# Convolution bands loaded from raw taps and softmaxed on the chip; small inputs asked for first

## The chip, the cores and the metric

The kernel runs on one core of a Trainium2 chip. The metric is the device time of one launch in microseconds, the median of several runs; lower is better. TensorE (PE) multiplies matrices, VectorE (DVE), ScalarE (ACT) and GpSimd (POOL) work element by element, SyncE (SP) issues most of the DMA transfers. ACT and POOL issue some as well, each on a queue of its own.

## What is computed

`x` is (8, 3584, 192), float32. A causal convolution with 7 taps runs along the sequence, with one set of taps for each of 8 heads of 24 channels; the taps are softmaxed first. Each of the 28672 rows then goes through one of 8 experts (192 to 1024 to 192, ReLU), which is chosen by a gate with a bias that depends on the row's modality.

```python
w = exp(weight - max(weight)); w = w / (sum(w) + 1e-9)         # (8 heads, 7 taps)
y[b, s, h] = sum_k w[h, k] * x_padded[b, s + k, h]             # causal: 6 zeros ahead
logits = y @ w_gate + modality_bias[modality_id]               # (28672, 8)
e = argmax(logits); gate = softmax(logits)[e]
out = gate * (relu(y @ w1[e]) @ w2[e])
```

## The kernel before

The sequence is cut into blocks of 120 positions for each of the 8 batches. 4 batches of a block are a quad, and 19 groups of 1, 2 or 4 quads go through the first stage. For one group: `x` is loaded with 128 positions on the partitions (120 and a halo of 8); the convolution is a matmul with a band matrix (`band`, 128x120 for each head, lines 336 to 374 of the listing of before: `convolve_pair` makes two heads at a time in one PSUM tile `cv`, which is copied to `y`). `turn` transposes `y` on DVE, `gate` multiplies it with the gate matrix (`gt`), `logits` adds the bias, `choose` takes the largest (`top`, `ex`, `rk`, `oh`), `place` counts the rows of each expert with matmuls (`rp`) and makes the row numbers `idx`, and `send` scatters the rows of `y` to a DRAM buffer sorted by expert (`routed_rows`), 120 rows in one instruction of POOL. The groups are laid out one behind the other by generators (`all_groups`, `body`, `finish`).

The second stage walks over slots of the sorted rows: a slot loads the weights of its expert, and each pass of 256 rows goes through `first` (`hps`) and `second` (`po`). Slot 0 starts when the rows of the first four groups (20 scatters) have landed; from there the later groups run between the steps of the second stage.

What lies around the change is the start. The framework sets the order on each engine from the program, and `issue_after` holds an instruction behind another on its engine. On SP stand, in this order: the taps, `x` of group 0, the line of tap weights, the band in two halves of four heads, `x` of group 1, and six more loads of `x` that wait for the band (`behind_band`). The taps are softmaxed on one partition (DVE and ACT), written into a zeroed line per head (`line`, in `raw1`), the line goes to DRAM (`tap_lines`), and the band is read back from there with a step of one element from partition to partition, so that each partition holds the taps one place further. `load_modality` asks for the modality ids on POOL; `make_gate` builds the gate matrix in two forms, `wg_whole` (in float32, for the groups below 8) and `wg_parts` (high and low halves, from group 8 on); `make_modality` turns the ids into `mt` (two transposes on PE into a PSUM tile of the same ring of four that `cv` uses, and a copy on DVE); `make_bias` makes `first_bias` from `mt` on POOL. POOL also clears the lower rows of the four `y` buffers (`clear`). `warm` keeps PE busy with matmuls of ones until the band is there.

Of the kernel before, what the change touches and what calls it, by code (L numbers as in the profile page):

```python
# [12 lines left out]
I32 = mybir.dt.int32  # L13
# [18 lines left out]
WARM = 34  # L32
WAIT = 3
PAD = 64
# [15 lines left out]
def conv_then_routed_ffn(ctx, tc, x, weight, modality, w_gate, mod_bias, w1, w2, out):  # L50
# [61 lines left out]

    spark = const.tile([1, 1], F32, name="spark")
# [27 lines left out]
    def make_bands():  # L141

        wide = P + MB
        line = raw1[0][0:1].rearrange("p c n -> p (c n)")[:, 0:H * wide].rearrange("p (h u) -> p h u", h=H)
        nc.vector.memset(line, 0.0)
        least = const.tile([1, H], F32, name="least")
        nc.vector.memset(least, 1e-9)
        taps = const.tile([1, H, K], F32, name="taps")
        nc.sync.dma_start(out=taps, in_=weight.unsqueeze(0))
        peak = const.tile([1, H], F32, name="peak")  # L150
        nc.vector.tensor_reduce(out=peak, in_=taps, axis=AX.X, op=ALU.max)
        nc.vector.tensor_tensor(out=taps, in0=taps, in1=peak.unsqueeze(2).broadcast_to([1, H, K]), op=ALU.subtract)
        nc.scalar.activation(out=taps, in_=taps, func=AF.Exp)
        tot = const.tile([1, H], F32, name="tot")
        nc.vector.tensor_reduce(out=tot, in_=taps, axis=AX.X, op=ALU.add)
        nc.vector.tensor_tensor(out=tot, in0=tot, in1=least, op=ALU.add)
        nc.vector.reciprocal(out=tot, in_=tot)

        first = MB - 1 + HALO - K + 1
# [20 lines left out]
    def make_gate():  # L180


        wg = const.tile([P, NK, E], F32, name="wg")
        for q in range(P // Q):
            nc.scalar.dma_start(out=wg[q * Q:(q + 1) * Q], in_=w_gate.rearrange("(k c) e -> c k e", c=Q))
# [4 lines left out]
        nc.gpsimd.memset(whole, 0.0)  # L190
        parts = const.tile([P, NK, P], F32R, name="wg_parts")
        nc.vector.tensor_copy(out=parts, in_=whole)
        for q in range(P // Q):
            rows = slice(q * Q, (q + 1) * Q)
            nc.vector.tensor_copy(out=whole[rows, :, q * Q:q * Q + E], in_=wg[rows])
            state["wg"] = nc.vector.tensor_copy(out=parts[rows, :, q * Q:q * Q + 2 * E], in_=f(wgs[rows])).ins
        return whole, parts

    def make_modality():
        both = const.tile([MB, 2, E], F32, name="both")  # L200
        nc.scalar.dma_start(out=both.rearrange("p m e -> p (m e)"),
                            in_=mod_bias.rearrange("m e -> (m e)").partition_broadcast(MB))
# [10 lines left out]
        with tc.issue_after(state["wg"]):  # L213
            nc.vector.tensor_copy(out=mt.rearrange("p b s -> p (b s)"), in_=mt_ps.rearrange("p q r -> p (q r)"))
# [3 lines left out]
    def load_modality():  # L218
        half = NB // 2
        each = half * NSB  # L220
        room = raw2[1].rearrange("p c d -> p (c d)")
        ids = room[0:each, 0:4 * MB].bitcast(I32).rearrange("p (q s) -> p q s", q=2)
        words = modality.bitcast(I32)
        nc.vector.memset(room[0:1, 0:2 * CUT], 0.0)

        def rows_of(b0, b1, sb0, q):
            at = 2 * ((q * half + b0) * S + sb0 * MB - CUT)
            n = NSB - sb0
            dims = [[2 * S, b1 - b0], [2 * MB, n], [1, 2 * MB]] if sb0 == 0 else [[2 * MB, n], [1, 2 * MB]]
            nc.gpsimd.dma_start(out=ids[b0 * NSB + sb0:b1 * NSB, q], in_=bass.AP(words.tensor, words.offset + at, dims))  # L230

        nc.gpsimd.dma_start(out=ids[0:1, 0, 2 * CUT:], in_=words[0:2 * (MB - CUT)].unsqueeze(0))
        rows_of(0, 1, 1, 0)
        rows_of(1, half, 0, 0)
        rows_of(0, half, 0, 1)
        return room, ids, each

    modality_rows = load_modality()
# [27 lines left out]
    def make_bias(dst, n, ids):  # L266
# [4 lines left out]
        nc.gpsimd.tensor_tensor(out=dst, in0=dst, in1=start_row.unsqueeze(1).broadcast_to([MB, n * nb, E]), op=ALU.add)  # L271
# [286 lines left out]
    def all_groups():  # L558
# [345 lines left out]
    for y in y_bufs[1:]:  # L904
        clear(y)
# [176 lines left out]
```

## Time and profile before

| | us |
|---|---|
| median of three runs (lowest, highest) | 1234.53 (1234.31, 1235.81) |
| the profiled execution | 1234.43 |
| its span, from the first instruction to the last | 1232.6 |
| PE busy in the span | 1211.1 (98%) |
| DVE, ACT, POOL busy | 967.9, 723.3, 528.7 |

The span begins with the first instruction. Times in the rows are microseconds from there. PE is counted as busy whenever a matmul is in flight, so its share tells that there is little air between matmuls, and not that each of them runs at its peak. The chain of the page, followed back from the last instruction, lies on PE for 84% of the span.

### The profile page before, as it was taken

To read this page: it belongs to the slowest core of one execution; us is meant where nothing else is said; L and a number is where in the kernel's file an instruction comes from. 1 tells how busy PE (TensorE), PEld (TensorE's weight loads), DVE (VectorE), ACT (ScalarE), POOL (GpSimd) and SP (SyncE) were. 2 spreads that over 40 slices of the span, in tenths; PEclk is the share of its full clock that TensorE was granted. 3 is DMA by queue.
4 is the path that set the end of the run, shared out by engine and by line. 5 is a ranking of instruction groups with operands and counts; after the bars stand their busy time and mean duration, and the time that the engine had idled before them with its cause. 6 is when DMAs were issued, how large, how long until landed. Compare 5 with 4: busy or idle time off the path is not lost.

```text
span 1232.6 us, 27980 instructions
## 1 busy us (share of the span) xinstructions
PE 1211.1 (98%) x9220; PEld 1196.6 (97%) x9220; DVE 967.9 (79%) x2455; ACT 723.3 (59%) x1588; POOL 528.7 (43%) x549
## 2 busy tenths in 40 slices
PE   9899999999999999999999999999999999999996
PEld 7799999999999999999999999999999999999995
DVE  6788986888788888788778887777766666787894
ACT  2366655565666556666655666555555555566773
POOL 7756564636344343545445344344352122112221
PEclk9999999999999999999999999999999999999998
DMA  8897563345544354345532554233262344943271
GB/s 222 221 224 211 122 179 77 77 116 142 134 88 111 84 125 110 72 107 142 143 63 57 109 121 126 53 71 61 73 158 56 81 106 106 258 112 94 42 191 38
DMA packets 308448, 144.29 MB, mean 117 GB/s; under 512 B 222922, under 2 KB 294930, under 8 KB 308293
## 3 DMA queue, kind: packets, MB, share of 16 engines
q1 hardware_dynamic: 284574, 97.83, 36.7%
q0 software_dynamic: 22752, 44.54, 11.6%
q8 instruction: 74, 1.21, 0.4%
q14 instruction: 81, 0.66, 0.2%
q10 hardware_dynamic: 967, 0.03, 0.0%
HBM read 116.58 MB, written 51.82 MB: 137 GB/s over the span
## 4 chain that ended last, share of the span: by engine, by line
PE 84%; DVE 6%; DMA 3%; issue 3%; ACT 1%; POOL 1%; SPq 0%; POOLq 0%; DVEq 0%; ACTq 0%
PE hps L835 39%; PE po L855 25%; PE po L859 12%; PE gt L405 3%; PE cv L349 3%; PE cv L365 2%; DMA routed_rows<-y,idx 1%; DVE hl L839 1%; DVE w1b L110 1%; DMA xr<-in_x_dram 1%; ACT lowp L871 1%; DVE xl L110 1%; DVE w2b L110 1%; POOL out_dram L874 0%; DVE sxs L822 0%
## 5 line engine op out<-in xcount | busy, mean ns | idle before, releaser
L855 PE MATMUL po<-w2b,hh 128*128 128x384 f32 x1824 | 556.3, 355 | 0.0
L835 PE MATMUL hps<-sxh,w1b 128*128 128x256 f32 x1824 | 482.0, 287 | 3.2 <-DVE hl L839 2.0
L839 DVE SCALAR_TENSOR_TENSOR hl<-hps,hh 128x512 fp32r<-128x512 f32 x456 | 312.0, 686 | 193.9 <-ACT hh L838 191.2
L838 ACT ACTIVATE hh<-hps 128x512 fp32r<-128x512 f32 x456 | 272.7, 598 | 324.6 <-PE hps L835 319.1
L859 PE MATMUL po<-w2b,hl 128*128 128x192 f32 x1824 | 443.4, 253 | 0.0
L874 POOL DMA_INDIRECT out_dram<-o,tags x228 | 236.5, 1037 | 382.5 <-DVE o L873 320.3
L251 POOL DMA_INDIRECT routed_rows<-y,idx x240 | 262.3, 1093 | 300.4 <-DVE hl L839 146.8
L835 PE MATMUL hps<-sxs,w1b 128*128 128x256 f32 x1824 | 363.5, 281 | 0.4 <-DVE sxs L822 0.4
L835 PEld LDWEIGHTS hps<-sxh,w1b 128*128 128x128 f32 x1824 | 344.8, 189 | 8.5 <-DVE hl L839 8.0
L859 PEld LDWEIGHTS po<-w2b,hl 128*128 128x128 f32 x1824 | 346.2, 191 | 0.0
L855 PEld LDWEIGHTS po<-w2b,hh 128*128 128x128 f32 x1824 | 344.3, 189 | 0.7 <-DVE o L873 0.4
L835 PEld LDWEIGHTS hps<-sxs,w1b 128*128 128x128 f32 x1824 | 280.0, 189 | 0.7 <-issue 0.7
L835 PE MATMUL hps<-sxl,w1b 128*128 128x256 f32 x912 | 256.3, 281 | 0.0
L835 PEld LDWEIGHTS hps<-sxl,w1b 128*128 128x128 f32 x912 | 173.0, 190 | 0.0
L110 DVE TENSOR_TENSOR w1b<-raw,w1b 128x512 fp32r<-128x512 f32 x152 | 101.3, 676 | 6.2 <-ACT w1b L108 5.9
L871 ACT ACTIVATE lowp<-po,tags 128x192 f32<-128x192 f32 x228 | 83.5, 417 | 30.9 <-PE po L855 30.8
L108 ACT CAST w1b<-raw 128x512 fp32r<-128x512 f32 x152 | 92.8, 621 | 3.4 <-DMA raw<-in_moe_w_dram 2.6
L110 DVE TENSOR_TENSOR w2b<-raw,w2b 128x384 fp32r<-128x384 f32 x152 | 80.9, 542 | 8.0 <-ACT w2b L108 7.6
L873 DVE SCALAR_TENSOR_TENSOR o<-po,tags,lowp 128x192 f32<-128x192 f32 x228 | 84.5, 412 | 2.2 <-ACT lowp L871 2.2
L820 ACT CAST sxs<-tp 64x128 fp32r<-64x128 f32 x224 | 66.7, 298 | 30.1 <-DVE tp L795 27.4
L108 ACT CAST w2b<-raw 128x384 fp32r<-128x384 f32 x152 | 75.9, 512 | 1.1
L822 DVE TENSOR_TENSOR sxs<-tp,sxs 64x128 fp32r<-64x128 f32 x224 | 64.8, 289 | 8.6
(158 smaller groups left out, 966.4 us busy)
## 6 DMA issues: line engine op xcount, KB each, us to landing
raw<-in_moe_w_dram SPq DMA_DIRECT2D x38, 768.0 KB
raw<-in_moe_w_dram SPq DMA_DIRECT2D x38, 512.0 KB
raw<-in_moe_w_dram SPq DMA_DIRECT2D x76, 256.0 KB
near<-routed_rows SPq DMA_DIRECT2D x208, 64.0 KB
xr<-in_x_dram SPq DMA_DIRECT2D x32, 384.0 KB
x<-in_x_dram SPq DMA_DIRECT2D x26, 384.0 KB
routed_rows<-filler SPq DMA_DIRECT2D x9, 776.0 KB
far<-routed_rows SPq DMA_DIRECT2D x208, 32.0 KB
```

The lines of the kernel that those rows point to most:

```text
L108: nc.scalar.copy(out=hi, in_=raw)
L110: return nc.vector.tensor_tensor(out=lo, in0=raw, in1=f(hi), op=ALU.subtract).ins
L251: state["scatter"] = nc.gpsimd.indirect_dma_start(out=scr, out_offset=bass.IndirectOffsetOnAxis(ap=idx, axis=0), in_=src, in_offset=None,).ins
L820: nc.scalar.copy(out=hi, in_=raw)
L835: nc.tensor.matmul(hps[:, u, :], wa[:, c, fs], mv[z], start=n == 0, stop=n == len(terms) - 1)
L838: nc.scalar.activation(out=hh, in_=hps, func=AF.Relu)
L839: hl_ins = nc.vector.scalar_tensor_tensor(out=hl, in0=hps, scalar=0.0, in1=f(hh), op0=ALU.max, op1=ALU.subtract)
L855: nc.tensor.matmul(po, hh[:, u, js], wb[:, c, :], start=c == 0, stop=c == NF - 1, skip_group_check=True)
L859: nc.tensor.matmul(po[:, 0:D], hl[:, u, js], wb[:, c, 0:D], start=False, stop=False, skip_group_check=True)
L871: nc.scalar.activation(out=lowp, in_=po[:, D:2 * D], func=AF.Copy, scale=gate)
L873: turn_behind(nc.vector.scalar_tensor_tensor(out=o, in0=po[:, 0:D], scalar=gate, in1=lowp, op0=ALU.mult, op1=ALU.add))
L874: st = nc.gpsimd.indirect_dma_start(out=out, out_offset=bass.IndirectOffsetOnAxis(ap=tag.bitcast(I32)[:, j, 1:2], axis=0), in_=o, in_offse ...
```

## The change

The ids, the taps, the gate matrix and the biases are asked for ahead of all else: the ids on POOL, the other three on ACT. The line in DRAM no longer holds softmaxed taps between zeros. It holds the raw weights, copied from DRAM to DRAM, between values of -1e30 that come from a small tile on 8 partitions (`outer`). The band is read from it in four parts of two heads. On the chip each head then goes through an exponential with minus the largest tap as bias (`peak`, ACT, in place), and each pair of heads is multiplied with one over the sum (`tot`, DVE). For that the taps are also loaded to all 128 partitions, where `peak` and `tot` are made. The padding turns to zero in the exponential.

`mt` is copied behind the last of these multiplications, the four copies into `wg_whole` stand behind `mt`, and `wg_parts` is made when group 5 is laid out, behind the row numbers that are newest there. The three clears of `y` stand behind `first_bias`. There are 28 warm matmuls, and 34 before.

```diff
-WARM = 34
+WARM = 28
+PARTS = 5
...
+    modality_rows = load_modality()
+
+    taps = const.tile([P, H, K], F32, name="taps")
+    nc.scalar.dma_start(out=taps.rearrange("p h k -> p (h k)"), in_=weight.rearrange("h k -> (h k)").partition_broadcast(P))
+    wg = const.tile([P, NK, E], F32, name="wg")
+    for q in range(P // Q):
+        state["wg"] = nc.scalar.dma_start(out=wg[q * Q:(q + 1) * Q], in_=w_gate.rearrange("(k c) e -> c k e", c=Q)).ins
+    both = const.tile([MB, 2, E], F32, name="both")
+    nc.scalar.dma_start(out=both.rearrange("p m e -> p (m e)"), in_=mod_bias.rearrange("m e -> (m e)").partition_broadcast(MB))
     spark = const.tile([1, 1], F32, name="spark")
...
     def make_bands():
...
+        first = MB - 1 + HALO - K + 1
+        each = first + K
+        outer = raw1[0][0:H, 0, 0:first]
+        nc.vector.memset(outer, -1e30)
+        lines = nc.dram_tensor("tap_lines", (H, 2 * each), F32, kind="Internal").ap()
+        nc.sync.dma_start(out=lines[:, first:each], in_=weight)
+        nc.sync.dma_start(out=lines.rearrange("h (two u) -> h two u", two=2)[:, :, 0:first],
+                          in_=outer.unsqueeze(1).broadcast_to([H, 2, first]))
+        band = xp.tile([P, H, MB], F32, name="band", tag="xr_0")
+        for h in range(0, H, 2):
+            part = bass.AP(lines.tensor, h * 2 * each, [[1, P], [2 * each, 2], [1, MB]])
+            state["band"] = nc.sync.dma_start(out=band[:, h:h + 2], in_=part).ins
+        peak = const.tile([P, H], F32, name="peak")
...
-        state["line"] = nc.vector.tensor_tensor(out=line[:, :, first:first + K], in0=taps,
-                                                in1=tot.unsqueeze(2).broadcast_to([1, H, K]), op=ALU.mult).ins
-        lines = nc.dram_tensor("tap_lines", (H, wide), F32, kind="Internal").ap()
-        nc.sync.dma_start(out=lines.unsqueeze(0), in_=line)
-        band = xp.tile([P, H, MB], F32, name="band", tag="xr_0")
-        for q in range(2):
-            part = bass.AP(lines.tensor, q * H // 2 * wide, [[1, P], [wide, H // 2], [1, MB]])
-            state["band"] = nc.sync.dma_start(out=band[:, q * H // 2:(q + 1) * H // 2], in_=part).ins
+        state["line"] = nc.vector.reciprocal(out=tot, in_=tot).ins
+        for h in range(H):
+            nc.scalar.activation(out=band[:, h], in_=band[:, h], func=AF.Exp, bias=peak[:, h:h + 1])
+            if h % 2:
+                pair = slice(h - 1, h + 1)
+                state["tuned"] = nc.vector.tensor_tensor(out=band[:, pair], in0=band[:, pair], in1=tot[:, pair].unsqueeze(2).broadcast_to([P, 2, MB]), op=ALU.mult).ins
...
     def make_gate():
...
+        with tc.issue_after(state["mt"]):
+            for q in range(P // Q):
+                rows = slice(q * Q, (q + 1) * Q)
+                nc.vector.tensor_copy(out=whole[rows, :, q * Q:q * Q + E], in_=wg[rows])
...
+        def make_parts():
+            with tc.issue_after(state["idx"]):
+                nc.vector.tensor_copy(out=parts, in_=whole)
+            for q in range(P // Q):
+                rows = slice(q * Q, (q + 1) * Q)
+                nc.vector.tensor_copy(out=parts[rows, :, q * Q:q * Q + 2 * E], in_=f(wgs[rows]))
...
-        with tc.issue_after(state["wg"]):
-            nc.vector.tensor_copy(out=mt.rearrange("p b s -> p (b s)"), in_=mt_ps.rearrange("p q r -> p (q r)"))
+        with tc.issue_after(state["tuned"]):
+            state["mt"] = nc.vector.tensor_copy(out=mt.rearrange("p b s -> p (b s)"), in_=mt_ps.rearrange("p q r -> p (q r)")).ins
...
         for g in range(NG):
+            if g == PARTS:
+                state["parts_of_gate"]()
...
-    for y in y_bufs[1:]:
-        clear(y)
+    with tc.issue_after(state["bias"]):
+        for y in y_bufs[1:]:
+            clear(y)
```

Three places show how the instructions stand. The first is DVE from the cast of the ids on (`raw`), through `mt`, to the first transposed `y` (`turned`); `y_182` of before and `y_179` of the change are the same buffer. Before:

```order
L208 CAST raw_1_88<-raw_1_88 120x240
L192 CAST wg_parts<-wg_whole 128x768
L195 COPY wg_whole<-wg 32x6x8
L196 CAST wg_parts<-wgs 32x6x16
...
L214 COPY mt<-mt_ps 120x240
L370 COPY y_182<-cv 120x2x4x24
L385 STREAM_TRANSPOSE turned<-y_182 128x4x6x32
L370 COPY y_182<-cv 120x2x4x24
L412 STREAM_TRANSPOSE lt<-gt 128x128
```

And in the change:

```order
L245 CAST raw_1_88<-raw_1_88 120x240
L202 TENSOR_TENSOR band<-band,tot 128x240 x3
L620 COPY base_240<-carry_177 1x8
L202 TENSOR_TENSOR band<-band,tot 128x240
L251 COPY mt<-mt_ps 120x240
L226 COPY wg_whole<-wg 32x6x8 x4
L386 COPY y_179<-cv 120x2x4x24
L401 STREAM_TRANSPOSE turned<-y_179 128x4x6x32
L386 COPY y_179<-cv 120x2x4x24
L401 STREAM_TRANSPOSE turned<-y_179 128x4x6x32
L428 STREAM_TRANSPOSE lt<-gt 128x128
```

The multiplications of the band and the copies into `wg_whole` now stand around `mt`, `wg_parts` is gone from here, and the transpose of group 1's `y` stands ahead of the first `lt`.

The second is PE behind the transposes of the ids: the convolutions of groups 0 and 1 (120x96), the gate of group 0, and the counting of group 0. Before:

```order
L211 MATMUL mt_ps<-ident,raw_1_88 120x120 x2
L365 MATMUL cv<-x,band 120x96 x14
L405 MATMUL gt<-turned,wg_whole 128x128 x6
L365 MATMUL cv<-x,band 120x96 x2
L365 MATMUL cv<-x,band 120x192 x4
L405 MATMUL gt<-turned,wg_whole 128x128 x3
L463 LDWEIGHTS tri
```

And in the change:

```order
L248 MATMUL mt_ps<-ident,raw_1_88 120x120 x2
L381 MATMUL cv<-x,band 120x96 x16
L421 MATMUL gt<-turned,wg_whole 128x128 x6
L381 MATMUL cv<-x,band 120x192 x2
L421 MATMUL gt<-turned,wg_whole 128x128 x5
L479 LDWEIGHTS tri
```

All of group 1's convolution now stands ahead of group 0's gate, and nearly all of group 1's gate ahead of group 0's counting. One row here is two matmuls in the profile, since float32 goes through PE in two passes.

The third is POOL from `first_bias` to the first scatter. Before:

```order
L242 MEMSET y_183 32x1552
L268 TENSOR_TENSOR first_bias<-mt,step 120x384
L242 MEMSET y_184 32x1552
L271 TENSOR_TENSOR first_bias<-first_bias,both 120x384
L242 MEMSET y_185 32x1552
L706 IOTA filler 128x1
L448 IOTA y_182 120x4
L268 TENSOR_TENSOR bt<-mt,step 120x128 x2
L271 TENSOR_TENSOR bt<-bt,both 120x128 x2
L251 DMA routed_rows<-y_182,idx 238592x194 x4
```

And in the change:

```order
L284 TENSOR_TENSOR first_bias<-mt,step 120x384
L724 IOTA filler 128x1
L464 IOTA y_179 120x4
L284 TENSOR_TENSOR bt<-mt,step 120x128
L287 TENSOR_TENSOR first_bias<-first_bias,both 120x384
L258 MEMSET y_180 32x1552
L258 MEMSET y_181 32x1552
L258 MEMSET y_182 32x1552
L287 TENSOR_TENSOR bt<-bt,both 120x128
L284 TENSOR_TENSOR bt<-mt,step 120x128
L287 TENSOR_TENSOR bt<-bt,both 120x128
L267 DMA routed_rows<-y_179,idx 238592x194 x4
```

The three clears have moved behind `first_bias`, so that all three stand behind `mt` and ahead of the first scatter.

## Rows read from the trace of the kernel before

**Rows 1.** Windows: from:to, length, busy (count) PE PEld DVE ACT POOL, clock, DMA, GB/s.

```profile
0.00:62.00 62.00, 55.63 (x392) 48.68 (x392) 45.76 (x208) 19.39 (x52) 47.02 (x65) 0.97 0.81 222
...
900.00:1200.00 300.00, 299.24 (x2306) 297.73 (x2304) 224.20 (x523) 186.29 (x404) 73.58 (x73) 1.00 0.51 117
```

**Rows 2.** Timeline, from row numbers to slot 0: start, duration, engine, line, idle before.

```profile
20.42 0.13 DVE L487 CAST idx<-row 120x4 int32<-120x4 f32 x1
...
21.54 1.10 POOL L251 DMA_INDIRECT routed_rows<-y,idx  x1 [3.10 <-ACT lg L438]
...
46.88 0.99 POOL L251 DMA_INDIRECT routed_rows<-y,idx  x1 [0.30 <-issue]
...
50.98 0.97 SPq L771 DMA_DIRECT2D raw<-routed_rows  x2
...
56.68 0.50 PE L835 MATMUL hps<-sxh,w1b 128*128 128x256 f32 x2
```

**Rows 3.** Timeline of SP's transfers, and GB/s in 40 slices of 0:16.

```profile
1.23 0.35 SPq L317 DMA_DIRECT2D x<-in_x_dram  x1
4.85 0.24 SPq L163 DMA_DIRECT2D tap_lines<-raw  x1
7.19 0.95 SPq L167 DMA_DIRECT2D band<-tap_lines  x2
8.18 0.47 SPq L317 DMA_DIRECT2D x<-in_x_dram  x1
...
GB/s 0 0 0 0 9 47 109 142 285 229 94 49 78 57 85 130 98 72 0 0 0 125 145 151 202 316 332 243 212 190 102 10 54 46 156 380 369 373 365 309
```

**Rows 4.** Timeline and chain of PE: warm matmuls, convolutions, first gate.

```profile
1.16 8.90 PE L125 MATMUL hps<-ones 120*120 120x480 bf16 x34 [1.16 <-DVE ones L120]
...
10.77 1.05 PE L365 MATMUL cv<-x,band 128*120 128x96 f32 x8 [0.51 <-issue]
12.00 1.08 PE L365 MATMUL cv<-x,band 128*120 128x96 f32 x8 [0.18 <-DMA band<-tap_lines]
13.43 1.47 PE L365 MATMUL cv<-x,band 128*120 128x96 f32 x12 [0.35 <-ACT y L368]
14.73 1.53 PE L405 MATMUL gt<-turned,wg_whole 128*128 128x128 f32 x12
...
16.75 1.53 PE cv L365 x8
```

**Rows 5.** DVE: timeline, and line L195 as minimum/median/maximum in ns.

```profile
8.10 0.61 DVE L192 CAST wg_parts<-wg_whole 128x768 fp32r<-128x768 f32 x1
...
L195 DVE COPY wg_whole<-wg x4: 177/181/1335, 8.7 to 10.7; 32x48 f32<-32x48 f32 x4
...
11.08 0.41 DVE L214 COPY mt<-mt_ps 120x240 f32<-120x240 f32 x1
...
13.46 0.98 DVE L385 STREAM_TRANSPOSE turned<-y 128x768 f32<-128x768 f32 x1 [0.41 <-ACT y L368]
...
18.74 0.19 DVE L441 TENSOR_TENSOR oh<-rk,first 120x32 bf16<-120x32 f32 x1
```

**Rows 6.** POOL: line L242 as minimum/median/maximum in ns, and timeline.

```profile
L242 POOL MEMSET y<- x4: 1387/1387/1690, 4.5 to 15.1; 32x1552 f32 x4
...
11.65 0.91 POOL L268 TENSOR_TENSOR first_bias<-mt,step 120x384 f32<-120x384 f32 x1 [1.61 <-DVE mt L214]
...
14.09 1.00 POOL L271 TENSOR_TENSOR first_bias<-first_bias,both 120x384 f32<-120x384 f32 x1
```

**Rows 7.** Timeline of ACT: an exponential of 120 partitions by 128.

```profile
57.11 0.31 ACT L438 ACTIVATE lg<-ex 120x128 f32<-120x128 f32 x1
```

**Rows 8.** Windows around a drop of PE's clock, columns as in Rows 1.

```profile
34.00:36.00 2.00, 0.86 (x4) 0.67 (x5) 2.00 (x23) 1.00 (x3) 1.70 (x2) 1.00 0.34 91
36.00:40.00 4.00, 2.68 (x19) 2.59 (x19) 3.27 (x18) 0.00 (x0) 2.99 (x4) 0.83 0.92 260
40.00:44.00 4.00, 4.00 (x24) 4.00 (x23) 1.94 (x11) 0.74 (x2) 3.14 (x4) 0.74 1.01 249
```

More of the change, by code (lines that the diff above doesn't have):

```diff
@@ L110, in split, with load_modality, rows_of @@
             return nc.vector.tensor_tensor(out=lo, in0=raw, in1=f(hi), op=ALU.subtract).ins
+    def load_modality():
+        half = NB // 2
+        each = half * NSB
+        room = raw2[1].rearrange("p c d -> p (c d)")
+        ids = room[0:each, 0:4 * MB].bitcast(I32).rearrange("p (q s) -> p q s", q=2)
+        words = modality.bitcast(I32)
+        nc.vector.memset(room[0:1, 0:2 * CUT], 0.0)
+        def rows_of(b0, b1, sb0, q):
+            at = 2 * ((q * half + b0) * S + sb0 * MB - CUT)
+            n = NSB - sb0
+            dims = [[2 * S, b1 - b0], [2 * MB, n], [1, 2 * MB]] if sb0 == 0 else [[2 * MB, n], [1, 2 * MB]]
+            nc.gpsimd.dma_start(out=ids[b0 * NSB + sb0:b1 * NSB, q], in_=bass.AP(words.tensor, words.offset + at, dims))
+        nc.gpsimd.dma_start(out=ids[0:1, 0, 2 * CUT:], in_=words[0:2 * (MB - CUT)].unsqueeze(0))
+        rows_of(0, 1, 1, 0)
+        rows_of(1, half, 0, 0)
+        rows_of(0, half, 0, 1)
+        return room, ids, each
+    modality_rows = load_modality()
[6 more added lines that the diff above has]
+    nc.scalar.dma_start(out=both.rearrange("p m e -> p (m e)"), in_=mod_bias.rearrange("m e -> (m e)").partition_broadcast(MB))
     spark = const.tile([1, 1], F32, name="spark")
@@ L141, in make_bands @@
     def make_bands():
[L143 to L146, printed above, removed]
-        nc.vector.memset(least, 1e-9)
[L148 to L151, printed above, removed]
@@ new lines, in make_bands @@
+        peak = const.tile([P, H], F32, name="peak")
+        nc.vector.tensor_reduce(out=peak, in_=taps, axis=AX.X, op=ALU.max)
+        nc.vector.tensor_scalar(out=peak, in0=peak, scalar1=-1.0, scalar2=None, op0=ALU.mult)
+        nc.vector.tensor_tensor(out=taps, in0=taps, in1=peak.unsqueeze(2).broadcast_to([P, H, K]), op=ALU.add)
+        with tc.issue_after(state["wg"]):
+            nc.scalar.activation(out=taps, in_=taps, func=AF.Exp)
+        tot = const.tile([P, H], F32, name="tot")
+        nc.vector.tensor_reduce(out=tot, in_=taps, axis=AX.X, op=ALU.add)
@@ new lines, in make_bands @@
+        least = const.tile([P, H], F32, name="least")
+        nc.vector.memset(least, 1e-9)
+        nc.vector.tensor_tensor(out=tot, in0=tot, in1=least, op=ALU.add)
+        state["line"] = nc.vector.reciprocal(out=tot, in_=tot).ins
[4 more added lines that the diff above has]
+                state["tuned"] = nc.vector.tensor_tensor(out=band[:, pair], in0=band[:, pair], in1=tot[:, pair].unsqueeze(2).broadcast_to([P, 2, MB]), op=ALU.mult).ins
@@ L180, in make_gate @@
     def make_gate():
-        wg = const.tile([P, NK, E], F32, name="wg")
-        for q in range(P // Q):
-            nc.scalar.dma_start(out=wg[q * Q:(q + 1) * Q], in_=w_gate.rearrange("(k c) e -> c k e", c=Q))
         wgs = const.tile([P, NK, 2 * E], F32R, name="wgs")
@@ L190, in make_gate @@
         nc.gpsimd.memset(whole, 0.0)
+        with tc.issue_after(state["mt"]):
+            for q in range(P // Q):
+                rows = slice(q * Q, (q + 1) * Q)
+                nc.vector.tensor_copy(out=whole[rows, :, q * Q:q * Q + E], in_=wg[rows])
         parts = const.tile([P, NK, P], F32R, name="wg_parts")
[L192 to L196, printed above, removed]
+        def make_parts():
[4 more added lines that the diff above has]
+                nc.vector.tensor_copy(out=parts[rows, :, q * Q:q * Q + 2 * E], in_=f(wgs[rows]))
+        state["parts_of_gate"] = make_parts
         return whole, parts
     def make_modality():
-        both = const.tile([MB, 2, E], F32, name="both")
-        nc.scalar.dma_start(out=both.rearrange("p m e -> p (m e)"),
-                            in_=mod_bias.rearrange("m e -> (m e)").partition_broadcast(MB))
         step = const.tile([MB, E], F32, name="step")
@@ L270, in make_bias @@
             in1=step.unsqueeze(1).unsqueeze(1).broadcast_to([MB, n, nb, E]), op=ALU.mult)
-        nc.gpsimd.tensor_tensor(out=dst, in0=dst, in1=start_row.unsqueeze(1).broadcast_to([MB, n * nb, E]), op=ALU.add)
+        state["bias"] = nc.gpsimd.tensor_tensor(out=dst, in0=dst, in1=start_row.unsqueeze(1).broadcast_to([MB, n * nb, E]), op=ALU.add).ins
     def behind_band(ins):
```

26 lines of the change are left out of this document (1 added, 25 removed).

## The prediction

> **What bounds the kernel now.** I read the windows by stage first. From 900 to 1200 us PE is busy 299.2 of 300 us; in the first 62 us it misses 6.4 us [rows 1]. So the second stage is PE's own work, which the change does not touch, and all that can be won or lost is when that stage begins. Next I read the timeline of the start. Slot 0 begins with its first product at 56.68, behind a load that SP issues at 50.98, behind the 20 scatters of the first four groups [rows 2]. The first of these starts at 21.54 and the 20th at 46.88, 19 steps of 1.33 us, and the later one waited only for its own issue [rows 2]. From 21.54 on POOL is thus the pace, and the path before it is: band in SBUF, convolution, gate, counting, row numbers (ready at 20.55), first scatter 1.0 us later [rows 2]. A microsecond won at the first scatter is a microsecond at the end, if the next scatters find their row numbers. Before the scatter, the chain is one of transfers: the line is issued at 4.85, the band at 7.19, its second half is used at 12.00 [rows 3, 4].
>
> **The change, part by part.** I follow the last pair of heads.
>
> *The line.* The softmax on one partition, which held the line's issue until 4.85, is gone from the path. The pads are issued when SP is through with `x` of group 0, at 1.23 + 0.35 = about 1.6 [rows 3]. From issue to the next issue such a write took 7.19 - 4.85 = 2.3 us, which puts the band's issue at 3.9 at the earliest. But the pads stand on SP's queue right behind 312 KB of `x`, where the line before found an emptied queue. The traffic peaks at 285 GB/s in the slice from 3.2 and is down to 49 in the one from 4.4 [rows 3]; if the write only begins then, it ends at 4.4 + 2.3 = 6.7. Between the two: half a band (240 KB) took 10.77 - 7.19 = 3.6 us from issue to use, so 312 KB takes some 4.2 and `x` lands at 5.4, with the small pads close behind, since transfers that are queued overlap (the second half of the band follows the first by 1.2 us and not by another 3.6) [rows 3, 4]. I take 5.4 for the band's issue, and keep 3.9 and 6.7.
>
> *The band.* Same bytes in four parts: from its first issue to the use of its last part 12.00 - 7.19 = 4.8 us [rows 3, 4]. It is there at 10.2 (8.7 to 11.5), 1.8 us earlier than before.
>
> *The softmax on the chip.* For the last pair two exponentials of 128x120, 0.31 each by the nearest row [rows 7], and a multiplication of 240 elements, which I price at the 0.41 of the copy of `mt` (240 elements too) [rows 5]: 1.0 us, usable at 11.2. The earlier pairs' work hides under the transfers. Then `mt`, now behind the last multiplication, ends at 11.6, where before it ended at 11.49 [rows 5]. The last pair of group 0 waits for that too, since its PSUM tile is the one that the transposed ids leave (a ring of four). So its convolution starts at 11.7; before, it was the second half of the matmuls from 12.00, at 12.54. Of 1.8 us 0.85 is left (2.3 with the early end, -0.45 with the late one).
>
> *Group 1 ahead of the gate.* The four pairs of group 1 take 0.54 each [rows 4]: 12.2 + 4 x 0.54 = 14.4. Their `x` is issued behind the band, about 1 us earlier than 8.18 [rows 3], and was used at 13.43 [rows 4], so 12.4 covers it. The gate of group 0 begins at 14.4 instead of 14.73, and ends at 15.9. On DVE `turned` of group 0 must be done by then: `mt` 11.6, four copies into `wg_whole` at 0.18 [rows 5] to 12.3, a copy of `y`, the transpose 0.98 [rows 5]: 13.7. That cover is 0.7 us.
>
> *Choosing and counting.* Before, from the end of the gate (16.26) to the end of `oh` (18.93) pass 2.7 us, with group 1's 0.98 us transpose in between [rows 4, 5]. The change puts that transpose ahead of `lt`, under the gate. `oh` is done at 15.9 + 1.7 = 17.6. But PE has a pair of group 2 (half of 1.53, so 0.77) and ten of twelve matmuls of group 1's gate (1.3) in between [rows 4]; the counting starts at 18.0, where before it could start at 18.93. That is 0.95 us won, and two more small DVE steps (0.2 each) now stand among those to `idx`: about 0.7 is left. First scatter at 20.85.
>
> *POOL.* `first_bias` starts 0.16 us after `mt`, then follow 0.91, 1.00, three clears of 1.39 [rows 6], four products and sums a third as long, at some 0.45 each as an estimate from those two, and small steps: 8.6 us from `mt`, so POOL is free at 20.2. Nothing is lost as long as `mt` ends before 12.2; beyond that each microsecond costs one.
>
> *`wg_parts` later.* 0.61 us and four casts of about 0.18 [rows 5] move from a stretch in which DVE waited anyway to the middle of the scatters. On DVE they cost nothing, since the row numbers of group 3 are ready long before their scatters. On POOL they can cost between nothing and 1.35 us, if a scatter must stand still for each of them. The trace shows such a meeting: while POOL cleared a buffer, one copy of `wg_whole` took 1335 ns instead of 181, and one clear took 1690 instead of 1387 [rows 5, 6]. I take 0.2, as short casts mostly fall into POOL's own issue gaps.
>
> The Trainium skill (SBUF — State Buffer, section "Who interferes with whom") says that GpSimd and a VectorE copy or cast in a two-port mode hold a shared port one at a time, and that descriptors which GpSimd makes for a DMA starve meanwhile. The trace agrees as to the copy and the clear; whether a scatter starves no row of mine shows. By that rule all five casts would be paid, 1.35 us instead of 0.2.
>
> *At no cost.* The ids, the gate matrix and the biases come earlier, but `mt` is no longer what they hold back. Six warm matmuls fewer (0.26 each on average) end the warm-up at 8.5 instead of 10.06 [rows 4], and nothing on PE waits for that: the first pair is ready no earlier than about 9. The filler's place on SP changes no wait of PE.
>
> **The sum.** -0.7 + 0.2 = -0.5 us. The profiled execution took 1234.43 (span 1232.6, 1.8 around it) and stands 0.1 below the median of 1234.53; I apply the sum to the median: 1234.0.
>
> **Rivals.**
>
> *Faster: the pads do not wait for `x`.* With the band's issue at 3.9 the band is in at 8.7, `mt` ends at 10.1, the last pair starts at 10.2, the gate at 12.9, the counting at 16.5; 2.4 us are won there, 2.2 at `idx`, and POOL is free at 18.7, ahead of the scatter. With the 0.2 lost: 1232.5, and 1231.5 if the last transfers and steps also run closer than in my bounds. For it: the pads are tiny. Against it: they share SP's queue with `x`.
>
> *Scatters stand still for the casts.* The full 1.35 us instead of 0.2: 1234.53 - 0.7 + 1.35 = 1235.2. For it is the 1335 ns copy [rows 5]; against it, that scatters at other places run at 0.99 next to a busy DVE. The rule of the Trainium skill named above would give this.
>
> *Slower: PE loses its clock.* PE is fed pair by pair from about 9 to 12, with gaps. The trace shows what a gap can do: in 34 to 36 PE was busy 0.86 of 2 us, and from 36 to 44 the granted clock was 0.83 and 0.74, part of that at 1.2 GHz instead of 2.4 [rows 8]. That is 4 x 0.17 + 4 x 0.26 = 1.7 us of clock. There it stood beside POOL's pace and cost nothing; here it would lie on the path, before the first scatter: 1234.0 + 1.7 = 1235.7, and with a second drop, or with `mt` late by the 6.7 end as well (POOL free at 21.5 instead of 20.2), 1237.2. It decides only if the gap is as long as that of 34 to 36; three pairs of 0.54 in 3 us make it about half busy. Against it: the warm matmuls reach to 8.5.
>
> *Nothing moves.* If DVE or POOL take up the 0.7, the time is 1234.5, inside the forecast's own width.
>
> **How the numbers follow.** Forecast (1233.2 to 1234.8): 0.60. Early pads: 0.17, around 1232.4. Casts in the scatters: 0.13, around 1235.2. PE's clock: 0.10, 1235.7 to 1237.2. A measurement of this kernel can tell about 0.2% from no change, 2.5 us: 1232.1 to 1237.0. Beyond the lower bound lies some 0.10 of the early pads and 0.03 of the forecast (a larger gain than I see), beyond the upper 0.06 of the clock and 0.01 of the casts. So faster 0.13, same 0.80, slower 0.07. The range leaves out 0.1 at each side: 1231.9 to 1236.2.
>
> **What would show it.** The band's first issue on SP: at 5.4 by the forecast, at 3.9 if the pads are free of `x`. The end of `mt` at 11.6, PE's first gate at 14.4, the first scatter at 20.85, the 20th at 46.2, slot 0's first product at 56.2. Granted clock 1.0 up to 34 us; a value below that between 10 and 22 is the slow rival. Scatters between 30 and 40 that take more than 0.99, next to the cast of `wg_parts`, are the casts. The forecast is wrong in its ground if the first scatter comes 2 us earlier and the end does not, or if the stage behind 62 us changes its length by itself.

## The result, and the profile of the changed kernel

The changed kernel takes 1247.47 us (1246.51 to 1249.26) against 1234.74 of the kernel before in the same comparison: a ratio of 1.0103, 95% interval [1.0089, 1.0116]. It is slower by 12.7 us, where I forecast 1234.0 and a range up to 1236.2. The span of its profiled execution is 1244.7 against 1232.6.

The windows tell where to look. The stretch from 900 to 1200 us is what it was, with PE busy 299.47 of 300 us. In the first 62 us PE is busy 48.84 us instead of 55.63, at a granted clock of 0.90 instead of 0.97 [rows 1]. Windows of the changed kernel; the columns are those of [rows 1]:

```profile
0.00:62.00 62.00, 48.84 (x319) 43.29 (x320) 40.01 (x188) 19.06 (x52) 43.81 (x63) 0.90 0.73 200
900.00:1200.00 300.00, 299.47 (x2311) 298.44 (x2310) 222.20 (x525) 183.21 (x396) 78.06 (x77) 1.00 0.51 119
```

Timeline of the changed kernel, in the order of [rows 3] to [rows 5] and then [rows 2]:

```profile
1.72 0.41 SPq L333 DMA_DIRECT2D x<-in_x_dram  x1
2.17 0.77 SPq L180 DMA_DIRECT2D tap_lines<-raw  x1
7.64 1.95 SPq L185 DMA_DIRECT2D band<-tap_lines  x4
10.66 1.25 ACT L199 ACTIVATE band<-band,peak 128x120 f32<-128x120 f32 x4 [2.00 <-DMA band<-tap_lines]
12.45 1.28 ACT L199 ACTIVATE band<-band,peak 128x120 f32<-128x120 f32 x4 [0.55 <-DMA band<-tap_lines]
...
14.09 0.40 DVE L251 COPY mt<-mt_ps 120x240 f32<-120x240 f32 x1
14.40 1.70 DVE L226 COPY wg_whole<-wg 32x48 f32<-32x48 f32 x4
...
11.88 7.04 PE L381 MATMUL cv<-x,band 128*120 128x96 f32 x32 [1.65 <-issue]
18.71 1.73 PE L421 MATMUL gt<-turned,wg_whole 128*128 128x128 f32 x12
...
24.10 0.16 DVE L503 CAST idx<-row 120x4 int32<-120x4 f32 x1
...
25.25 1.11 POOL L267 DMA_INDIRECT routed_rows<-y,idx  x1 [2.68 <-ACT y L384]
...
50.76 0.99 POOL L267 DMA_INDIRECT routed_rows<-y,idx  x1 [0.30 <-issue]
...
68.34 0.50 PE L853 MATMUL hps<-sxh,w1b 128*128 128x256 f32 x2
```

There are two losses. The first scatter comes at 25.25 instead of 21.54 [rows 2], 3.7 us late. From there to slot 0's first product pass 68.34 - 25.25 = 43.1 us instead of 56.68 - 21.54 = 35.1, another 8.0. After that no more than 0.4 us is added. The second loss does not lie in the scatters, since 19 steps take 50.76 - 25.25 = 25.51 us instead of 25.34. Nor is it anything that I had priced. It shows in SP's loads of `x` and in PE's work on group 7. In the timeline before:

```profile
34.89 0.98 SPq L320 DMA_DIRECT2D x<-in_x_dram  x2
52.57 1.10 SPq L320 DMA_DIRECT2D x<-in_x_dram  x2
...
52.29 0.81 PE L365 MATMUL cv<-x,band 128*120 128x192 f32 x4
52.94 2.84 PE L405 MATMUL gt<-turned,wg_whole 128*128 128x128 f32 x24
```

And in that of the changed kernel:

```profile
39.02 0.37 SPq L336 DMA_DIRECT2D x<-in_x_dram  x1
54.51 0.97 SPq L789 DMA_DIRECT2D raw<-routed_rows  x2
55.68 0.37 SPq L789 DMA_DIRECT2D tags<-routed_rows  x1
56.10 1.91 SPq L336 DMA_DIRECT2D x<-in_x_dram  x3
...
53.34 2.84 PE L421 MATMUL gt<-turned,wg_whole 128*128 128x128 f32 x24
61.11 1.60 PE L381 MATMUL cv<-x,band 128*120 128x192 f32 x4 [4.93 <-DMA x<-in_x_dram]
62.51 4.94 PE L421 MATMUL gt<-turned,wg_whole 128*128 128x128 f32 x24
```

The loads of `x` in these rows bring group 7, one load for each of its four quads. The first convolution of that group reads the first two quads. On PE it stands ahead of the second half of group 6's gate, and both stand ahead of slot 0's transposes. Before the change two of the four loads stood on SP ahead of slot 0's loads (34.89); now it is one (39.02). The second is behind `raw<-routed_rows`, which waits for the scatters, so it is issued at 56.10, and PE stands still for 4.93 us. Then the clock is at half: the 24 matmuls of the gate take 4.94 us where 24 of them took 2.84 ahead of the stall.

Two sets of the runs below (e5 to e7, and e11 with e12) fell on two chips on which all kernels, the one before among them, took 32 to 37 us longer, with PE standing still for up to 10 us between 30 and 80 us, so their times are compared only within their set (marked as on a slow chip).

### The profile page after: what moved, and what is told of

The parts are those of the page before. It is cut to its first block, busy times and chain, and to the rows that moved or that the text cites. A ratio compares the mean times of both kernels' runs of the same rounds, so it can differ in the third digit from the quotient of the medians.

```text
span 1244.7 us, 27988 instructions
## 1 busy us (share of the span) xinstructions
PE 1215.5 (98%) x9214; PEld 1201.8 (97%) x9214; DVE 969.2 (78%) x2459; ACT 726.1 (58%) x1596; POOL 528.3 (42%) x549
## 4 chain that ended last, share of the span: by engine, by line
PE 84%; DVE 4%; issue 2%; DMA 2%; ACT 1%; SPq 1%; POOL 1%; DVEq 0%; POOLq 0%; ACTq 0%
PE hps L853 39%; PE po L873 25%; PE po L877 12%; PE gt L421 3%; PE cv L365 3%; PE cv L381 1%; DVE hl L857 1%; DMA xr<-in_x_dram 1%; ACT lowp L889 1%; DVE w1b L111 1%; DVE xl L111 1%; DMA near<-routed_rows 1%; DVE tp L811 0%; DMA routed_rows<-y,idx 0%; DVE o L891 0%
```

## The experiments

The theory has two parts: a load out of place (8 us), and a start in which the band comes late and PE loses its clock (3.7 us). The rivals stand with each experiment. The table gives, from the profiles, when the gate of group 0, the first scatter and slot 0's first product begin, and the time between the last two. Its last column is the median, beside that of the kernel before in the same set. "Load ahead" means that group 7's second load stands ahead of slot 0's loads, as before the change; "band first" means that the band stands ahead of `x` of group 0.

| kernel | gate | scatter | slot 0 | between | median (before) |
|---|---|---|---|---|---|
| before | 14.73 | 21.54 | 56.68 | 35.1 | 1234.5 |
| changed | 18.71 | 25.25 | 68.34 | 43.1 | 1247.5 (1234.7) |
| e1: changed, load ahead | 18.35 | 24.45 | 59.69 | 35.2 | 1238.5 (1234.4) |
| e2: before, load behind | 14.98 | 21.77 | 64.49 | 42.7 | 1242.7 (1234.4) |
| e13: before, 28 warm | 15.84 | 22.59 | 65.50 | 42.9 | 1243.6 (1234.9) |
| e3: changed, 36 warm | 17.75 | 24.02 | 64.01 | 40.0 | 1243.8 (1234.4) |
| e4: changed, pads first | 16.34 | 22.59 | 64.70 | 42.1 | 1243.1 (1234.4) |
| e10: changed, band first | 17.01 | 23.22 | 63.08 | 39.9 | 1243.9 (1234.7) |
| e9: e1 and 36 warm | 17.41 | 23.69 | 59.35 | 35.7 | 1237.0 (1234.7) |
| e8: e1 and band first | 16.74 | 23.15 | 58.15 | 35.0 | 1237.1 (1234.7) |
| e14: all three | 15.54 | 21.47 | 56.62 | 35.2 | 1234.6 (1234.9) |

**e1, the load put back.** Slot 0's loads are laid out 14 steps later in the program, which puts group 7's second load ahead of them again. PE, ACT and POOL keep the order of the changed kernel; on DVE a few small steps change places.

```diff
-        bring(lots.index((i, 0)))
+        if i:
+            bring(lots.index((i, 0)))
...
+            if n == 14:
+                bring(0)
             advance()
```

> The changed kernel with one load moved back: the second x load of group 7 stands again ahead of slot 0's loads on SP, as before the change; PE, ACT and POOL keep the order of the changed kernel, DVE swaps a few small steps of the table. Theory (a load behind slot 0's loads stalls PE): of the 11.6 us lost at slot 0's first product about 8 are this load, 4.9 us of PE standing still at 61.1 in the changed kernel and 3.4 us of clock at 60 to 67 that follow from it. Then the time is 1239.5 (1238.5 to 1241) against 1247.5 of the changed kernel; slot 0's first product stands about 3.7 us behind that of the kernel before, as the first scatter does. Rival (all of it comes from the start, and the PE stall only fills time in which slot 0 would have waited for its rows anyway): 1246.5 to 1248, the stall reappears on the products of slot 0.

Measured 1238.54, ratio to before 1.0030 [1.0019, 1.0041]. Timeline:

```profile
38.15 0.92 SPq L336 DMA_DIRECT2D x<-in_x_dram  x2
...
55.30 0.81 PE L381 MATMUL cv<-x,band 128*120 128x192 f32 x4
55.95 2.84 PE L421 MATMUL gt<-turned,wg_whole 128*128 128x128 f32 x24
```

There are two loads in a row, no wait ahead of the convolution, a gate at full clock, and 35.2 us from scatter to slot 0, as before the change. The span is 1244.7 - 1236.5 = 8.2 us shorter, of the 12.1 between the spans of the changed kernel and the one before. The first scatter is 0.8 us earlier too (24.45 for 25.25); the load lies behind it and cannot do that, so what the load does is the 43.1 - 35.2 = 7.9 us between scatter and slot 0.

**e2, the load alone in the kernel before.** `KEPT + 1` is group 7 and `q` counts its quads: all its loads but the first are held behind slot 0's, and nothing else moves.

```diff
-            pin = "load" if self.g == KEPT + 2 else "x"
+            pin = "load" if self.g == KEPT + 2 or self.g == KEPT + 1 and q else "x"
```

> The kernel before with that one load moved the other way: the second x load of group 7 behind slot 0's loads on SP; every other engine has the same order as before. Theory (the load): PE stalls some 5 us ahead of slot 0's transposes, the granted clock falls after it, and the time is 1240 to 1243 against 1234.6. Rival (the load hurts only because the changed kernel's start is already late): 1234 to 1236.

Measured 1242.70, ratio 1.0069 [1.0056, 1.0082]. The start is that of the kernel before within 0.3 us, and the stall is there:

```profile
52.59 1.69 SPq L320 DMA_DIRECT2D x<-in_x_dram  x3
...
57.23 1.61 PE L365 MATMUL cv<-x,band 128*120 128x192 f32 x4 [4.73 <-DMA x<-in_x_dram]
58.62 4.96 PE L405 MATMUL gt<-turned,wg_whole 128*128 128x128 f32 x24
```

So the load needs no late start to do its harm.

**e12 and e13, one number.** Which edit moved the load? The framework works out the order on SP from times that it estimates, so an edit of the start can do it. In the kernel before, `WARM = 28` for 34 is enough.

> The kernel before with one number of the change alone, 28 instead of 34 warm matmuls. In the order of its loads on SP this alone puts the second x load of group 7 behind slot 0's loads, as in the changed kernel, since the order is worked out from estimated times. Theory (the load): PE stalls about 5 us ahead of slot 0's transposes and the time is 1241 to 1243.5, whatever the start does; a first scatter at 21.5 to 22.5, later than 21.54 if the gap behind the shorter warm-up costs the clock. Rival (six warm matmuls fewer are free, as I predicted): 1234 to 1236.

On a slow chip this gave 1264.68 against 1267.06 of the kernel before, a miss. The load was behind, yet PE came to the convolution without a wait, at 63.55, since other pauses had held it up before (5.24 us ahead of a gate at 45.58, waiting for DVE, among them). Of this run only the start is used.

> Once more the kernel before with 28 instead of 34 warm matmuls alone. On the slow chip of the first run its start could be read: half speed from 12.7 to 16.1, gate of group 0 at 16.57 instead of 14.73, first scatter at 23.30 instead of 21.54. Theory (this one number is most of the loss: 1.8 us through the clock at the start, and some 7 us more through group 7's load, which it moves behind slot 0's loads): 1243 (1241.5 to 1244.5) against 1234.6. Rival (the load costs nothing here, since the slow chip showed no loss at the end): 1235.5 to 1237.

Measured 1243.56, ratio 1.0073 [1.0058, 1.0088]. Windows of the start and of the stretch about the stall, and timeline:

```profile
10.00:20.00 10.00, 8.91 (x61) 8.61 (x62) 5.45 (x21) 3.02 (x9) 6.53 (x11) 0.83 0.90 262
56.00:63.00 7.00, 3.56 (x16) 3.59 (x17) 0.00 (x0) 0.00 (x0) 5.40 (x6) 0.52 1.04 318
```

```profile
10.97 5.03 PE L365 MATMUL cv<-x,band 128*120 128x96 f32 x30 [1.86 <-POOL y L242]
...
59.44 1.61 PE L365 MATMUL cv<-x,band 128*120 128x192 f32 x4 [5.86 <-DMA x<-in_x_dram]
```

One number that I had put down as free costs 8.7 us. Some 1.0 of it is at the first scatter: PE now stands idle for 1.86 us ahead of the first convolution, and the granted clock of 10 to 20 falls to 0.83. The other 7.8 lie between scatter and slot 0. The new order differs in more than the load (30 matmuls of convolution instead of 28 stand ahead of group 0's gate), so e13 shows what the number costs as a whole, and e2 what the load costs alone. The number is enough to move the load, but it is not the only edit that does: the changed kernel with 36 warm matmuls (e3, next) still stalls at it.

**e3 and e9, the clock of the start.** `WARM = 36` in the changed kernel (e3) and in e1 (e5, e9).

> The changed kernel with 36 instead of 28 warm matmuls, which at 0.26 us each end at about 11.4 instead of 9.3, just ahead of the first pair of heads at 11.85. Theory (PE loses its clock at the start because it stands idle from 9.8 to 11.85 and is then fed pair by pair): the clock stays at full speed between 10 and 20, the 6.8 us at half speed are gone, the gate of group 0 starts at about 17 instead of 18.7, the first scatter at 23.5 instead of 25.25, and the time is 1245.7 (1245 to 1246.5). Rival (the late band alone sets the start): the gate and the first scatter stay within 0.4 us and the time stays at 1247.5. A third way: the clock falls all the same, since the pairs come in pieces; then as the rival.

> Both repairs at once: group 7's second x load ahead of slot 0's loads, and 36 instead of 28 warm matmuls. With the load in its place PE has no stall near 60 us, so what the 8 warm matmuls give here is the clock of the start alone. Theory (clock at the start): granted clock 1.0 from 10 to 20, first scatter 23.3 to 24.0 instead of 24.45 of the kernel with the load alone, and 1237.6 (1237.0 to 1238.2) against 1238.5; the 3.7 us that the same edit gave without the load in its place were then mostly the clock after PE's stall. Rival (the start's clock costs 3.4 us or more by itself): first scatter below 22, 1235 to 1236.

> Once more the kernel with group 7's load in its place and 36 warm matmuls, for the same reason. Theory (the start's clock alone): granted clock 1.0 from 10 to 20, first scatter at 23.3 to 24.1, 1237.6 (1237.0 to 1238.2), about 0.9 below the kernel with the load alone. Rival: below 1236.5, if the clock of the start is worth more than its share of the first scatter.

Windows from 10 to 20, first in the changed kernel (with the 7 us about the end of its stall), then in e3, then in e9:

```profile
10.00:20.00 10.00, 8.24 (x44) 7.65 (x43) 5.99 (x14) 4.24 (x14) 5.37 (x8) 0.66 0.86 243
60.00:67.00 7.00, 5.89 (x26) 5.92 (x27) 0.51 (x2) 0.00 (x0) 5.34 (x6) 0.51 1.05 343
```

```profile
10.00:20.00 10.00, 8.37 (x60) 6.88 (x59) 6.66 (x16) 4.32 (x14) 5.25 (x8) 1.00 0.84 241
```

```profile
10.00:20.00 10.00, 8.04 (x59) 6.77 (x58) 6.94 (x18) 4.60 (x15) 5.60 (x8) 1.00 0.83 241
```

The stall in the timelines of e3 and, from the runs further down, of e10:

```profile
59.55 0.88 PE L381 MATMUL cv<-x,band 128*120 128x192 f32 x4 [3.59 <-DMA x<-in_x_dram]
60.27 2.84 PE L421 MATMUL gt<-turned,wg_whole 128*128 128x128 f32 x24
...
58.62 0.88 PE L384 MATMUL cv<-x,band 128*120 128x192 f32 x4 [3.47 <-DMA x<-in_x_dram]
59.34 2.84 PE L424 MATMUL gt<-turned,wg_whole 128*128 128x128 f32 x24
```

With 36 warm matmuls PE stands idle for 0.57 us (e3) and 0.52 us (e9) ahead of the first convolution, and the clock holds. The first scatter comes 0.8 us earlier in e9 than in e1, as forecast, and 1.2 earlier in e3 than in the changed kernel, where I had 1.75. e9 came to 1237.04 (forecast 1237.6), ratio 1.0019 [1.0010, 1.0028]. e3 came to 1243.81 (1241.34 to 1246.41), ratio 1.0080 [1.0067, 1.0093], 1.9 lower than I expected. In its profiled execution, the fastest of its five, the clock stayed up after the stall too, and the gate behind it took 2.84 us, not 4.94. e10 and e3, without the drop, need 39.9 and 40.0 us from scatter to slot 0; the changed kernel, e2 and e13 need 42.7 to 43.1. So of the load's 8 us some 5 are the stall and 3 the clock behind it. In e5, the kernel of e9 on a slow chip, the clock was at half from 14.9 to 18.3 all the same (first scatter 24.08, 1274.37 against 1271.88).

**e6, DVE's copies.** This is e5 with 34 warm matmuls, and with `mt` and the four copies into `wg_whole` ahead of the band's multiplications. The loop over the heads becomes a function `tune`, which is called behind `make_gate` and `make_modality`.

```diff
-        with tc.issue_after(state["tuned"]):
+        with tc.issue_after(state["whole"]):
             state["mt"] = ...
+                    with tc.issue_after(state["mt"]):
+                        nc.vector.tensor_tensor(out=band[:, pair], ...)
```

> The last kernel with 34 warm matmuls and with DVE's four copies into wg_whole and its copy of mt ahead of the band's multiplications, where DVE stands idle, instead of behind them; the other engines keep their order. Theory (with the clock up, the gate of group 0 waits for DVE: mt 0.40 and four copies that take 1.70 while POOL works on first_bias stand ahead of the transpose): the four copies take 0.7, the gate starts at 16.2 to 16.8 instead of 17.75, the first scatter at 22.3 to 22.9, and the time is 1236.3 (1235.6 to 1237). Rival (PE's convolutions or the band set the gate, and the copies are covered): gate and scatter within 0.4 us of the last kernel, 1237.5.

On a slow chip it gave 1274.48 against 1271.88, with the gate at 17.15 and the first scatter at 23.28: a miss. The copies became short, as foreseen, but the multiplications became long. Operations of DVE on the two tiles, as minimum/median/maximum in ns:

```profile
L205 DVE TENSOR_TENSOR band<-band,tot x4: 408/852/1130, 11.7 to 13.7; 128x240 f32<-128x240 f32 x4
...
L230 DVE COPY wg_whole<-wg x4: 170/178/184, 9.6 to 10.2; 32x48 f32<-32x48 f32 x4
```

In e9 the same multiplications took 409 to 410 ns and the copies up to 948. Whatever DVE does behind `mt` runs beside POOL's `first_bias`, which starts with `mt`. The Trainium skill (SBUF — State Buffer, section "Who interferes with whom") says that a DVE instruction with two inputs in SBUF contends with a GpSimd instruction that reads SBUF; the rows of the multiplications agree.

**e4, the pads ahead of `x` on SP.** The load of `x` of group 0 is held behind the write of the pads.

```diff
-        with tc.issue_after(state["band"]) if g >= BEFORE_BAND else nullcontext():
+        with tc.issue_after(state["band"] if g >= BEFORE_BAND else state["pads"]):
```

> The changed kernel with the pads' write ahead of the x load of group 0 on SP, where it stood behind; all engines but SP keep their order (one small copy of DVE moves). Theory (the pads land late because 312 KB of x stand ahead of them in the same queue): the band's first load is issued at 4.0 to 4.7 instead of 7.64, the band is in 3 us earlier, PE has no gap behind the warm matmuls and keeps its clock, the first scatter comes at 20.5 to 22.5 instead of 25.25, and the time is 1243 (1242 to 1245). Rival (a write of 16 short rows and its receipt take that long by themselves): the band is issued at 6.5 or later, and the time is 1246.5 to 1247.5.

Measured 1243.06, ratio 1.0069 [1.0056, 1.0082]. Timeline:

```profile
1.72 0.74 SPq L180 DMA_DIRECT2D tap_lines<-raw  x1
2.50 0.47 SPq L333 DMA_DIRECT2D x<-in_x_dram  x1
4.21 1.95 SPq L185 DMA_DIRECT2D band<-tap_lines  x4
...
9.96 2.39 ACT L199 ACTIVATE band<-band,peak 128x120 f32<-128x120 f32 x8 [0.33 <-DMA band<-tap_lines]
```

The write takes 2.5 us when nothing is ahead of it, and 5.5 behind `x`. But of the 3.4 us won at the band's issue only 0.7 arrive at the first exponential (9.96 for 10.66). Two things can hold it back here, and e4 does not part them. The band now travels beside `x`, and ACT first makes its cast of the gate matrix, which lands late too: that cast runs from 9.40 to 9.63, and the exponential then waits 0.33 us more for the band. All eight exponentials follow without a gap, and the scatter comes at 22.59. I had expected that the clock would hold; 10 to 20 stood at 0.83.

**e7, e8, e10: the whole band ahead of `x`.** `BEFORE_BAND = 0`, and the small steps on the gate matrix (ACT, DVE) and the biases (DVE) behind the band's; e7 and e8 with the load in its place, e10 without. The two edits were only tried together.

> The changed kernel with group 7's load in its place, the pads and the four parts of the band ahead of the x load of group 0 on SP, and with the steps on the gate matrix and the biases behind the band's on ACT and DVE. Theory (what the changed start loses is the queue: pads behind x, band beside x): the band's first load is issued at 4.2, the last part is there by 9 to 9.5 since no x shares the way, the last multiplication ends at 10 to 10.5, x of group 0 lands by 10.5, the gate starts at 14 to 15, the first scatter at 20.5 to 21.5, and the time is 1234.5 (1233.5 to 1235.5), level with the kernel before. Rival (the band's rows of 480 bytes are slow whatever stands beside them, or x of group 0 comes too late): the first convolution starts later than 10.8, the first scatter at 22.5 or later, 1236 or more.

> Once more the kernel with group 7's load in its place and the band ahead of x of group 0. The chip of the run before ran every kernel some 37 us longer, the kernel before too, with PE standing still for up to 10 us between 30 and 80 us without a wait that the profile shows, so only its first 25 us could be read: gate of group 0 at 14.84, first scatter at 20.94. Theory (from the first scatter on, the stage goes as before the change once the load is in its place): on a chip like that of the first runs the time is 1234.2 (1233.2 to 1235.2), no more than 0.1% off the kernel before, and slot 0's first product comes at 55.7 to 56.8. Rival (something else of the change still costs behind the first scatter, the casts of wg_parts between the scatters above all): 1236 or more with the first scatter on time.

> The changed kernel with the band ahead of x of group 0 and the gate's steps behind, but with group 7's second load left where the change put it, behind slot 0's loads. Theory (two independent losses that add): first scatter at 20.9, PE still stalls some 5 us ahead of slot 0's transposes, and the time is 1242.5 (1241 to 1244): 5 below the changed kernel, 8 above the one with both repairs. Rival (the misplaced load hurts only because the start is late): 1236 or less.

e7, on a slow chip, began as expected (gate 14.84, scatter 20.94), at 1273.77 against 1271.88. The first exponential of e8 began at 8.31, so with both edits the band's earlier issue does arrive. Yet e8 gave 1237.09, ratio 1.0017 [1.0008, 1.0026], 2.9 above its forecast, with the scatter at 23.15. PE stood idle for 1.85 us ahead of the first convolution at 11.71, and the clock of 10 to 20 was 0.83; in e7, the same kernel, the idle time was 1.53 us and the clock held. In e7, e10 and e14 the profile puts this wait down to `x`, in e8 to a small step of DVE. Behind the scatter e8 needs 35.0 us, so nothing of the change is left there. e10 gave 1243.85 (forecast 1242.5), with the scatter at 23.22 and not at the 20.9 forecast, and a stall of 3.47 us and not of 5. In spans, the load costs 1244.7 - 1236.5 = 8.2 with the late start and 1241.4 - 1234.0 = 7.4 with the better one, so the two losses add within a microsecond.

**e11 and e14, all three repairs**: e8 with `WARM = 36`.

> All three repairs in the changed kernel: group 7's second load ahead of slot 0's, the band ahead of x of group 0, and 36 warm matmuls, which end at about 11.6, when the first convolution can begin (11.7). Theory (what is left of the loss, 1.6 us at the first scatter, is the 3.4 us at half speed from 13.1): granted clock 1.0 from 10 to 20, gate of group 0 at 14.8 to 15.5 instead of 16.74, first scatter at 21.0 to 21.9, 1235.2 (1234.2 to 1236.0), level with the kernel before. Rival (the longer warm-up delays the first convolutions as much as the clock gives back, or another wait takes the clock's place): first scatter at 22.5 or later, 1237.

> Once more the changed kernel with all three repairs: load in its place, band ahead of x of group 0, 36 warm matmuls. On the slow chip its start showed no half speed before 30, gate at 15.26, first scatter at 21.48, and a time 1.9 us below the kernel before. Theory (the three are the whole loss): first scatter at 21.2 to 21.8, slot 0's first product 35.1 behind it, 1234.9 (1234.0 to 1235.8), level with the kernel before within 0.1%. Rival (there is a fourth loss): 1237.

e11, on a slow chip, gave 1265.19 against 1267.06. e14 gave 1234.63 against 1234.90, ratio 0.9998 [0.9989, 1.0006]. A window of e14 and its timeline:

```profile
10.00:20.00 10.00, 9.02 (x76) 8.31 (x75) 7.86 (x29) 3.33 (x11) 7.79 (x11) 1.00 1.07 295
```

```profile
12.05 3.65 PE L384 MATMUL cv<-x,band 128*120 128x96 f32 x32 [0.95 <-DMA x<-in_x_dram]
...
21.47 1.11 POOL L270 DMA_INDIRECT routed_rows<-y,idx  x1 [1.81 <-ACT y L387]
...
56.62 0.51 PE L856 MATMUL hps<-sxh,w1b 128*128 128x256 f32 x2
```

The 32 matmuls of convolution take 3.65 us, not 7.04, and the first scatter is where it was before. Load, clock, and the band behind `x` (together with the gate's small steps ahead of the band's) are the whole loss. The version is level with the kernel before and beats it by nothing that can be measured: here PE waits for `x`, where before it waited for the band.

## Why the prediction was wrong, step by step

*What bounds the kernel* held: with the load in its place slot 0 follows the first scatter by 35.0 to 35.7 us in all kernels, so a microsecond there is one at the end. That POOL is the pace from the first scatter on held only for these; with the load behind, PE's wait for `x` is the one that ends last ahead of slot 0.

*"The filler's place on SP changes no wait of PE."* This step failed, and it is 8 of the 12.7 us. The sum had nothing for the order on SP. I looked at the filler and did not follow the `x` loads behind it, of which one had moved behind slot 0's loads, and so behind the wait for the scatters: PE stood still for 4.93 us, and 3 us more went to the clock. No rival had it either. No line of the diff touches these loads; e13 shows that the number of warm matmuls is enough to move one.

*"Nothing on PE waits"* for six warm matmuls failed: e13 shows 1.0 us at the scatter and the moved load.

*PE loses its clock* was a rival with a chance of 0.10, and it came: 0.66 from 10 to 20, with 1.65 us idle ahead of the first pair. It is part of the 3.7 us at the first scatter. My price of 1.7 us was near (1.2 and 0.8 in e3 and e9, 1.7 from e8 to e14), the chance was not. I had leaned on the warm matmuls reaching to 8.5 and the first pair being ready at about 9; PE began it at 11.88.

*The line.* Forecast 5.4, kept ends 3.9 and 6.7, measured 7.64. That the pads wait for `x` was right, and e4 shows the other end (4.21). The size was wrong, in two ways. By its own row, 240 KB in 3.6 us, 312 KB come to 4.7 us and not to 4.2, so that the term would have been 5.9. And I took the traffic of before [rows 3] for a start in which taps for 128 partitions, gate matrix, biases and ids are all asked for ahead. Which of these holds the pads up was not tried.

*The band* took 12.45 - 7.64 = 4.8 us from first issue to the last wait for it, as forecast. That wait was for the third pair; when ACT came to the fourth, 0.6 us later, it was there. *The softmax on the chip*: from 12.45 to the end of `mt` pass 14.49 - 12.45 = 2.0 us, where I had 1.0 and 0.4. Four exponentials (1.28 us) stood behind the last wait and not two of 0.31 each [rows 7], then a multiplication of 0.41, as priced, and `mt`. So `mt` ended 2.9 us later than forecast, 2.2 of it from the line.

*The copies into `wg_whole`*: 1.70 us, not 4 x 0.18. The 1335 ns copy of [rows 5] was in my hands, and I used it for the scatters only. With the clock up they are on the path: in e9 they end at 15.89, a copy of `y` and the transpose follow on DVE, and the gate starts at 17.41, when the transpose is done.

*Gate to scatter, and POOL*, held: 25.25 - 18.71 = 6.5 us, where I had 20.85 - 14.4 = 6.45. The row numbers were ready at 24.26, and POOL had been free since 22.57.

*The casts between the scatters*: 0.2 us forecast, 0.17 measured over 19 steps. The rival of 1.35 is out. The scatter beside the cast of 0.54 us does take longer, but by 0.2 and not by the whole cast (changed kernel):

```profile
36.10 1.00 POOL L267 DMA_INDIRECT routed_rows<-y,idx  x1 [0.30 <-POOL y L464]
37.41 1.19 POOL L267 DMA_INDIRECT routed_rows<-y,idx  x1 [0.30 <-issue]
...
37.19 0.54 DVE L231 CAST wg_parts<-wg_whole 128x768 fp32r<-128x768 f32 x1
```

## What to carry to other kernels

Where a scheduler lays out the queues, read the whole order of each queue after any edit, down to the stage that matters. Ask of each load that moved what it now stands behind and who reads it first. An edit of the start can cost most at a place 50 us later. Work that only keeps PE's clock up is not free to shorten: its end has to meet the first real work.

## What the runs showed of the hardware

A write of 7.6 KB took 2.5 us from its issue to that of the transfer that waits for it when it stood ahead of 312 KB of `x` on the same queue (e4), and 5.5 behind them (changed kernel). Moving the write ahead won 3.4 us at the band's issue and 0.7 at the first use, with the band beside `x`. With `x` behind the band, and the gate's cast behind the exponentials, the first use came at 8.31 instead of 10.66 (e8).

The granted clock fell from 2.4 to 1.2 GHz in the start of the changed kernel, after 1.65 us of idle time of PE, and after its stall of 4.93 us. After stalls of 3.59 us (e3) and 3.47 us (e10) at the same place it did not fall; after 4.09 us (e4) it did, and the gate took 4.47 us. One kernel kept its clock in the start of one run, after 1.53 us idle (e7, on a slow chip), and lost it in another, after 1.85 us (e8): the first scatter came at 20.94 and at 23.15. Whether the stall ahead of slot 0 cost its own length or 3 us more depended on the clock.

A DVE multiplication of 128 x 240 took 0.41 us in e9 and up to 1.13 beside a POOL operation that reads SBUF (e6). POOL's own operation then took 1.14 us instead of 0.92.
